# Three small tables at the start of a fused attention and mixture-of-experts kernel: other order, other queue, and four clears moved

## The chip, the cores and the metric

The kernel runs on one core of one Trainium2 chip. Its engines are TensorE (PE: matmuls, with weight loads shown apart as PEld), VectorE (DVE), ScalarE (ACT), GpSimd (POOL) and SyncE (SP, which here only issues transfers). The metric is the device time of one execution in microseconds; lower is better. Before the change it was 571.02 us, the median of three runs (569.08 to 572.53).

## The reference, cut to what matters

Three stages follow one another: an attention layer with a bias computed from positions, a token and channel mixer, and a layer of eight experts. The change touches the attention's start only, where the bias is prepared.

```python
scale = 1.0 / np.sqrt(D)                       # B, H, S, D = 2, 8, 576, 64; HID = 32
scores = scale * np.matmul(q, k.transpose(0, 1, 3, 2))
psi_rel = np.log1p(np.abs(pos[:, None] - pos[None, :]))
psi_i = np.log1p(np.maximum(pos[:, None], 1.0))
x = (psi_rel / psi_i)[..., None]
h = np.maximum(x @ w1 + b1, 0.0)               # w1: [1, 32], b1: [32]
bias = h @ w2                                  # w2: [32, 8]
scores = scores + bias.transpose(2, 0, 1)[None]
attn = softmax(scores)                         # then attn @ v
x = mixer(attn @ v); out = experts(x)          # two more stages, not touched
```

## The kernel before, in words

The bias is made in groups of 16 query rows. For each group, four "hidden" tiles of 128 x 576 hold max(distance x scale, -b1): line 497 on VectorE or GpSimd, line 494 on ScalarE. TensorE then multiplies them with `wblk`, a 128 x 32 block-diagonal copy of w2 (line 507), ScalarE copies the sum out and adds a constant (`ev`, line 510), and SyncE's queue writes it into the bias tile (lines 516 and 518). Five groups are made before the first scores. After them come 40 attention steps (scores, softmax, transposes, values), the mixer and the experts.

What all groups need is loaded in `load_const`:
- `tabs` (line 180): the table of distances with its scales, 128 rows of 848 numbers, 424 KB; its rest follows in line 186.
- `w1c`, `b1c` and `w2r` (lines 181 to 183): w1, b1 and w2, each repeated four times over the 128 partitions, so one number, one number and eight numbers a partition.
- From `w2r` GpSimd builds `wblk` (a clear in line 194, four copies in line 197).
- From `b1c` VectorE makes `negb` (line 464), from `tabs` and `w1c` it makes `sc` (line 465). All hidden tiles wait for these two.
- `bias_const` (lines 479 and 481) multiplies `wblk` with `b1c` and copies four constants out, between the hidden tiles of the first group and those of the second.

The order of the work is written out by hand. The lists in `ORDER` name the steps in the order of issue, and `ENGINE` says which engine takes which copy; each engine then runs its instructions in that order and waits where data is missing. Transfers of SyncE go to one DMA queue (q1 in the profile) in the order of issue, those of ScalarE to another (q10). SyncE also waits: each transfer signals one of eight semaphores in turn, and a transfer is issued only when the earlier one on the same semaphore has landed. So the tail of the first keys (line 227) is the first that can wait, for the transfer issued first on that semaphore.

`query_zero` (lines 297 and 298) clears the parts of the two query buffers `qt` that no later copy writes. In the kernel before it is the step "zero" of the list "start", between hidden3 and key_T01.

Of the kernel before, what the change touches and what calls it, by code (L numbers as in the profile page):

```python
# [21 lines left out]
B, H, S, D = 2, 8, 576, 64  # L22
# [32 lines left out]
QO = 3, 3, 3, 6  # L55

ORDER = {
    "start": "hidden0 const load_k2 tail_split0 hidden1 bias0 hidden2 bias1 key_T00 hidden3 zero key_T01 key_T11 key_T10 key_split0 tail_split1 bias2 hidden4 bias3 load_k4 hidden5 key_split1 tail_T bias4 load_v load_q".split(),
    "first": "scores0 hidden2 last_T prob_T0 values key_T0 tail_T hidden0 normalize query_T query_split hidden1 key_T1 bias_mm key_split out_T tail_split hidden3 query_rest".split(),
    "mixed": "hidden2 scores0 values tail_T hidden0 query_T normalize last_T prob_T0 key_T0 key_T1 query_split tail_split hidden1 key_split bias_mm query_rest out_T hidden3".split(),  # L60
    "bias": "query_T query_split hidden3 scores0 scores1 last_T values hidden0 query_rest hidden2 late bias_mm out_T mix prob_T0 prob_T1 hidden1 normalize".split(),
# [47 lines left out]
def body(ctx, tc, q, k, v, w1, b1, w2, wt1, wt2, wc1, wc2, wg, wl, mw1, mw2,  # L109
# [17 lines left out]
    with tc.manual_schedule():  # L127
        tok = ctx.enter_context(ExitStack())
        mix = TokenMix(nc, x)
        attention(tc, nc, tok, mix, q, k, v, w1, b1, w2, c_L, c_id, ident, x, wt1, wt2, prefill)  # L130
        if "x" in dbg:
            nc.sync.dma_start(dbg["x"], x)
        R = Routing(tc, nc, wg, wl, ident, c_tok, c_small, x2d, meta)
        X = Experts(tc, nc, R, Rings(tc, ctx, "big", side="right"), x_p, mw1, mw2, ident, x2d, meta, out)
        mixer(tc, nc, tok, mix, wc1, wc2, ident, x, R, X)
        if "x2" in dbg:
            nc.sync.dma_start(dbg["x2"], x2d)
        X.rest()
        X.close()
        R.close()  # L140


def attention(tc, nc, tok, mix, q, k, v, w1, b1, w2, c_L, c_id, ident, x, wt1, wt2, prefill):
# [10 lines left out]
    with ExitStack() as ctx:  # L154
# [8 lines left out]
        def alloc_ps():  # L163
            return ps_t.tile([128, 512], F32, name="tp", tag="tr")
# [3 lines left out]
        w1c = cst.tile([128, 1], F32, name="w1c")  # L168
        b1c = cst.tile([128, 1], F32, name="b1c")
        w2r = cst.tile([128, H], F32, name="w2r")  # L170
        wblk = cst.tile([128, 32], F32, name="wblk")

        def load_const():
            four = lambda ap, n: ap.rearrange("(a k) o -> a k o", a=1).to_broadcast([4, HID, n])

            cut = 4 * NG + S + 128
            warm = cst.tile([128, 1], F32, name="warm")
            nc.vector.memset(warm, 0.0)
            nc.scalar.activation(warm, warm, AF.Exp)
            nc.sync.dma_start(tabs[:, 0:cut], c_L[:, 0:cut])  # L180
            nc.scalar.dma_start(w1c, four(w1.rearrange("o k -> k o"), 1))
            nc.sync.dma_start(b1c, four(b1.rearrange("(k o) -> k o", o=1), 1))
            nc.sync.dma_start(w2r, four(w2, H))
            load_k(0)
            load_q(*steps[0])
            nc.sync.dma_start(tabs[:, cut:], c_L[:, cut:])
            nc.sync.dma_start(ident, c_id)

            zero = x[:, 0]
            nc.vector.memset(zero, 0.0)  # L190
            ps = alloc_ps()
            for _ in range(WARM):
                nc.tensor.matmul(ps, lhsT=zero[:, 0:128], rhs=zero, start=True, stop=True)
            nc.gpsimd.memset(wblk, 0.0)
            for ii in range(4):
                r = slice(32 * ii, 32 * ii + 32)
                nc.gpsimd.tensor_copy(wblk[r, 8 * ii:8 * ii + 8], w2r[r])
# [22 lines left out]
        def load_k(i):  # L220

            b, pr = divmod(i, NP)
            n = nat_p.tile([128, 20, D], F32, name="kn", tag="kn", bufs=2)
            main, hs = n[:, 0:16].rearrange("p (n h) d -> p n h d", h=4), k[b, 2 * pr:2 * pr + 4]
            for j in range(NIT):
                nc.sync.dma_start(main[:, j], hs[:, 128 * j:128 * j + 128].rearrange("h p d -> p h d"))
            nc.sync.dma_start(n[0:64, 16:20], hs[:, 512:S].rearrange("h p d -> p h d"))
            for j in range(2):
                nat["k", i + j] = main[:, :, 2 * j:2 * j + 2], n[0:64, 16 + 2 * j:18 + 2 * j]
# [14 lines left out]
        def load_q(it, i):  # L244

            b, pr = divmod(i, NP)
            n = nat_p.tile([128, 4, D], F32, name="qn", tag="qn", bufs=2)
            if it == NIT:
                tv = q[b, :, 512:S].rearrange("(a e) p d -> e p a d", e=2)
                for e in range(2):  # L250
                    nc.sync.dma_start(n[64 * e:64 * e + 64], tv[e])
                for j in range(NP):
                    nat["q", it, i + j] = n[:, j]
            else:
                nc.sync.dma_start(n, q[b, 2 * pr:2 * pr + 4, 128 * it:128 * it + 128].rearrange("h p d -> p h d"))
                nat["q", it, i] = n
# [37 lines left out]
        def query_zero():  # L294

            for qt in qts:
                nc.gpsimd.memset(qt[:, :, 0:2, 64:128].bitcast(F32), 0.0)
                nc.gpsimd.memset(qt[:, :, 2:4, 0:64].bitcast(F32), 0.0)
# [329 lines left out]
        def late_fetch(s):  # L628

            if pieces and any(f is decode for f, *_ in late.get(s, ())):  # L630
                fetch(pieces.pop(0))

        load_const()
        bias_setup()
        start = {
            "const": (bias_const,), "zero": (query_zero,), "load_k2": (load_k, 2), "load_k4": (load_k, 4), "load_v": (load_v, 0),
            "load_q": (load_q, *steps[NP]), "tail_T": (tail_T, *steps[0]),
        }
        for n in range(2):
# [1151 lines left out]
```

## Time and profile before

| | before |
|---|---|
| median of three runs | 571.02 us (569.08 to 572.53) |
| the profiled execution | 570.33 us |
| its span, first to last instruction | 568.3 us |
| TensorE busy | 543.3 us, 96% of the span |
| VectorE, ScalarE, GpSimd busy | 67%, 58%, 43% of the span |
| mean granted TensorE clock | 0.992 of full speed |

The span is what the trace covers; 2.0 us of the profiled execution lie around it. Times in the rows below are counted from the span's start. The part that the change touches lies before the first scores, which start 20.14 us after it.

### The profile page before, as it was taken

To read this page: it belongs to the slowest core of one execution; us is meant where nothing else is said; L and a number is where in the kernel's file an instruction comes from. 1 tells how busy PE (TensorE), PEld (TensorE's weight loads), DVE (VectorE), ACT (ScalarE), POOL (GpSimd) and SP (SyncE) were. 2 spreads that over 40 slices of the span, in tenths; PEclk is the share of its full clock that TensorE was granted. 3 is DMA by queue.
4 is the path that set the end of the run, shared out by engine and by line. 5 is a ranking of instruction groups with operands and counts; after the bars stand their busy time and mean duration, and the time that the engine had idled before them with its cause. 6 is when DMAs were issued, how large, how long until landed. Compare 5 with 4: busy or idle time off the path is not lost.

```text
span 568.3 us, 11965 instructions
## 1 busy us (share of the span) xinstructions
PE 543.3 (96%) x4306; PEld 429.5 (76%) x4306; DVE 380.7 (67%) x886; ACT 332.0 (58%) x622; POOL 243.9 (43%) x236
## 2 busy tenths in 40 slices
PE   7899999999999999999999989999999999999992
PEld 3566777777778987789999867787778778787872
DVE  6788798989987864899888247523582136668650
ACT  5799898799897862544444132223422457777760
POOL 4676656566772440244444202300034054657541
PEclk9899999999999999999999999999999999999998
DMA  6794785665754430344442030271003974576950
GB/s 163 181 198 118 172 188 140 175 147 128 165 128 118 113 111 2 100 129 148 150 151 72 0 93 1 54 284 33 20 19 118 400 273 129 168 240 223 372 187 14
DMA packets 72416, 79.92 MB, mean 141 GB/s; under 512 B 37126, under 2 KB 51724, under 8 KB 72348
## 3 DMA queue, kind: packets, MB, share of 16 engines
q1 hardware_dynamic: 68924, 73.80, 45.4%
q0 software_dynamic: 2176, 5.26, 2.7%
q8 instruction: 36, 0.59, 0.5%
q14 instruction: 32, 0.26, 0.2%
q10 hardware_dynamic: 1248, 0.01, 0.1%
HBM read 72.08 MB, written 5.34 MB: 136 GB/s over the span
## 4 chain that ended last, share of the span: by engine, by line
PE 74%; DVE 10%; ACT 6%; issue 4%; DMA 2%; POOL 2%; SPq 0%; POOLq 0%; DVEq 0%; ACTq 0%
PE ph L770 20%; PE po L770 15%; PE tp L436 7%; PE ps L370 6%; PE py L770 5%; PE ps L507 5%; PE tp L421 5%; PE tp L770 1%; DVE t L348 1%; PE tp L1476 1%; DVE K L282 1%; DVE raw L754 1%; DMA bias<-ev 1%; ACT t L351 1%; PE tp L452 1%
## 5 line engine op out<-in xcount | busy, mean ns | idle before, releaser
L497 POOL TENSOR_SCALAR hd<-tabs,sc,negb 128x576 f32<-128x576 f32 x32 | 76.3, 2388 | 3.1 <-PE tp L452 1.8
L770 PE MATMUL po<-cw,h 128*128 128x512 f32 x272 | 67.3, 396 | 0.0
L351 ACT ACTIVATE t<-t,st 128x576 f32<-128x576 f32 x72 | 55.4, 771 | 18.1 <-DVE st L348 17.7
L348 DVE CUSTOM_DVE_ANT_0 t<-ps,bias 128x576 f32<-128x576 f32 x72 | 52.2, 750 | 7.9 <-PE ps L370 5.2
L1439 DVE TENSOR_TENSOR big<-raw,big 128x1024 fp32r<-128x1024 f32 x30 | 42.5, 1438 | 22.2 <-ACT big L1438 22.1
L770 PEld LDWEIGHTS po<-cw,h 128*128 128x128 f32 x272 | 49.8, 188 | 10.0 <-issue 0.4
L370 PE MATMUL ps<-K,qt 128*128 128x288 f32 x320 | 54.8, 312 | 2.0 <-DVE qt L209 1.6
L436 PE MATMUL tp<-pt,v 128*64 128x128 f32 (+1 forms) x800 | 49.3, 268 | 0.0
L1217 POOL DMA_INDIRECT meta<-tokid,posi x10 | 10.0, 998 | 90.3 <-DVE tokid L1214 54.4
L370 PEld LDWEIGHTS ps<-K,qt 128*128 128x128 f32 x320 | 45.2, 192 | 4.0 <-POOL t L362 2.1
L770 PE MATMUL py<-big,hT 128*128 128x512 f32 x184 | 47.8, 400 | 0.4 <-POOL big L1439 0.4
L507 PE MATMUL ps<-hd,wblk 128*32 128x288 f32 x576 | 44.2, 412 | 2.5 <-DVE st L348 1.0
L1438 ACT CAST big<-raw 128x1024 fp32r<-128x1024 f32 x44 | 44.3, 1056 | 2.8 <-DMA big<-in_moe_w_dram 1.0
L436 PEld LDWEIGHTS tp<-pt,v 128*64 128x64 f32 x800 | 40.2, 137 | 7.4 <-issue 5.1
L770 PE MATMUL ph<-big,xT 128*128 128x512 f32 x168 | 42.9, 403 | 0.0
L497 DVE TENSOR_SCALAR hd<-tabs,sc,negb 128x576 f32<-128x576 f32 x69 | 42.3, 643 | 0.1
L762 POOL TENSOR_TENSOR big<-wf,big 128x512 fp32r<-128x512 f32 x12 | 18.7, 1558 | 51.1 <-ACT big L761 51.1
L770 PEld LDWEIGHTS py<-big,hT 128*128 128x128 f32 x184 | 33.8, 188 | 8.6 <-POOL big L1439 0.8
L494 ACT ACTIVATE hd<-tabs,b1c,sc 128x576 f32<-128x576 f32 x43 | 37.0, 866 | 3.8 <-DVE sc L465 3.7
L1439 POOL TENSOR_TENSOR big<-raw,big 128x1024 fp32r<-128x1024 f32 x10 | 27.6, 2763 | 24.3 <-ACT big L1438 24.3
L770 PEld LDWEIGHTS ph<-big,xT 128*128 128x128 f32 x168 | 30.6, 189 | 8.6 <-issue 1.6
L421 PE MATMUL tp<-ident,t 128*128 128x128 f32 x256 | 34.2, 275 | 0.0
(304 smaller groups left out, 1189.1 us busy)
## 6 DMA issues: line engine op xcount, KB each, us to landing
raw<-in_moe_w_dram SPq DMA_DIRECT2D x48, 512.0 KB
raw<-in_moe_w_ch_dram SPq DMA_DIRECT2D x24, 512.0 KB
bias<-ev SPq DMA_DIRECT2D x32, 288.0 KB
qt<-qs SPq DMA_DIRECT2D x64, 128.0 KB
lw<-in_moe_w_dram SPq DMA_DIRECT2D x16, 512.0 KB
big<-in_moe_w_dram SPq DMA_DIRECT2D x8, 512.0 KB
lw<-in_moe_w_dram SPq DMA_DIRECT2D x16, 256.0 KB
big<-in_moe_w_dram SPq DMA_DIRECT2D x16, 256.0 KB
```

What stands on the lines that cost most here:

```text
L348: nc.vector.tensor_tensor_reduce(t.rearrange("p (a j) -> p a j", a=2), ps[:, :, 0:HALF], bs.rearrange("p (a j) -> p a j", a=2), op0=ALU.ad ...
L351: nc.scalar.activation(t, t, AF.Exp, bias=st[:, j:j + 1], scale=-1.0, accum_out=st[:, 2 + j:3 + j])
L370: nc.tensor.matmul(ps[:, hf, 0:HALF], lhsT=qt[:, j], rhs=K[k][:, hf * HALF:(hf + 1) * HALF], start=j == pairs[0][0], stop=j == pairs[-1][0])
L421: nc.tensor.transpose(tp[:, 128 * j:128 * j + 128], tt[:, o:o + 128], ident)
L436: nc.tensor.matmul(po[64 * h:64 * h + 64, 0:rhs.shape[1]], lhsT=lhsT, rhs=rhs, start=j == 0, stop=j == 4)
L494: nc.scalar.activation(hd[:, qq], Lt[:, o:o + S], AF.Relu, bias=b1c, scale=sc[:, c])
L497: eng.tensor_scalar(hd[:, qq], Lt[:, o:o + S], sc[:, c], negb, ALU.mult, ALU.max)
L507: nc.tensor.matmul(ps[32 * qq:32 * qq + 32, hf, 0:HALF], lhsT=wblk, rhs=hd[:, qq, hf * HALF:(hf + 1) * HALF], start=True, stop=True)
L762: nc.gpsimd.tensor_tensor(lo, src, hi.bitcast(F32), ALU.subtract)
L770: nc.tensor.matmul(out, lhsT=lhs[a], rhs=rhs[b], start=first and i == 0, stop=last and i == 2)
L1438: nc.scalar.copy(hi, raw)
L1439: (nc.gpsimd if c == 3 and t else nc.vector).tensor_tensor(lo, raw, hi.bitcast(F32), ALU.subtract)
```

## The change

The transfer of `b1c` is issued first on SyncE's queue and `tabs` second. `w2r` leaves SyncE's queue for ScalarE's, behind `w1c`. `query_zero` is called at GpSimd's first instruction of the kernel, ahead of the clear of `wblk`, and no longer stands in the list "start".

```diff
-    "start": "hidden0 const load_k2 tail_split0 hidden1 bias0 hidden2 bias1 key_T00 hidden3 zero key_T01 key_T11 key_T10 key_split0 tail_split1 bias2 hidden4 bias3 load_k4 hidden5 key_split1 tail_T bias4 load_v load_q".split(),
+    "start": "hidden0 const load_k2 tail_split0 hidden1 bias0 hidden2 bias1 key_T00 hidden3 key_T01 key_T11 key_T10 key_split0 tail_split1 bias2 hidden4 bias3 load_k4 hidden5 key_split1 tail_T bias4 load_v load_q".split(),
...
             nc.vector.memset(warm, 0.0)
             nc.scalar.activation(warm, warm, AF.Exp)
+            nc.sync.dma_start(b1c, four(b1.rearrange("(k o) -> k o", o=1), 1))
+            nc.scalar.dma_start(w1c, four(w1.rearrange("o k -> k o"), 1))
             nc.sync.dma_start(tabs[:, 0:cut], c_L[:, 0:cut])
-            nc.scalar.dma_start(w1c, four(w1.rearrange("o k -> k o"), 1))
-            nc.sync.dma_start(b1c, four(b1.rearrange("(k o) -> k o", o=1), 1))
-            nc.sync.dma_start(w2r, four(w2, H))
+            nc.scalar.dma_start(w2r, four(w2, H))
             load_k(0)
...
                 nc.tensor.matmul(ps, lhsT=zero[:, 0:128], rhs=zero, start=True, stop=True)
+            query_zero()
             nc.gpsimd.memset(wblk, 0.0)
...
-            "const": (bias_const,), "zero": (query_zero,), "load_k2": (load_k, 2), "load_k4": (load_k, 4), "load_v": (load_v, 0),
+            "const": (bias_const,), "load_k2": (load_k, 2), "load_k4": (load_k, 4), "load_v": (load_v, 0),
```

On SyncE's queue the program begins with these transfers before the change (`kn` are the keys, `qn` the queries):

```order
L180 DMA tabs<-in_c_L_dram 128x848
L182 DMA b1c<-in_b_dram 128x1x1
L183 DMA w2r<-in_w_dram 128x1x8
L226 DMA kn<-in_k_dram 128x4x64 x4
L227 DMA kn<-in_k_dram 64x4x64
L251 DMA qn<-in_q_dram 64x4x64 x2
```

With the change they stand as follows; line numbers below line 193 are higher by one.

```order
L180 DMA b1c<-in_b_dram 128x1x1
L182 DMA tabs<-in_c_L_dram 128x848
L227 DMA kn<-in_k_dram 128x4x64 x4
L228 DMA kn<-in_k_dram 64x4x64
L252 DMA qn<-in_q_dram 64x4x64 x2
```

`b1c` went ahead of `tabs`, and `w2r` left; ScalarE now issues it directly behind `w1c`, and everything else on both engines keeps its order. On GpSimd the first work of the program before the change is this (`hd` is a hidden tile, `qm` the split queries):

```order
L194 MEMSET wblk 128x32
L197 COPY wblk<-w2r 32x8 x4
L203 CAST qm<-qn 128x2x64
L305 ISA
L305 TENSOR_TENSOR qm<-qn,qm 128x64
L497 TENSOR_SCALAR hd<-tabs,sc,negb 128x576
L297 MEMSET qt_104 128x2x2x64
L298 MEMSET qt_104 128x2x2x64
L297 MEMSET qt_105 128x2x2x64
L298 MEMSET qt_105 128x2x2x64
```

With the change it is this:

```order
L298 MEMSET qt_104 128x2x2x64
L299 MEMSET qt_104 128x2x2x64
L298 MEMSET qt_105 128x2x2x64
L299 MEMSET qt_105 128x2x2x64
L195 MEMSET wblk 128x32
L198 COPY wblk<-w2r 32x8 x4
L204 CAST qm<-qn 128x2x64
L306 ISA
L306 TENSOR_TENSOR qm<-qn,qm 128x64
L498 TENSOR_SCALAR hd<-tabs,sc,negb 128x576
```

The four clears moved ahead of everything that waits for a transfer. On TensorE and VectorE no instruction changes its place.

## Rows read from the trace of the kernel before

**Rows 1.** The page's first lines: span; busy time of each engine, share, instructions.

```profile
span 568.3 us, 11965 instructions
PE 543.3 (96%) x4306; PEld 429.5 (76%) x4306; DVE 380.7 (67%) x886; ACT 332.0 (58%) x622; POOL 243.9 (43%) x236
```

**Rows 2.** VectorE's timeline, 5 to 20: start us, us, instructions [idle before <-releaser].

```profile
5.51 0.15 DVE L464 TENSOR_SCALAR negb<-b1c 128x1 f32<-128x1 f32 x1 [4.06 <-DMA b1c<-in_b_dram]
5.60 0.29 DVE L465 TENSOR_SCALAR sc<-tabs,w1c 128x144 f32<-128x144 f32 x1
5.93 2.05 DVE L497 TENSOR_SCALAR hd<-tabs,sc,negb 128x576 f32<-128x576 f32 x4
7.91 0.44 DVE L481 COPY cb<-tp 128x1 f32<-128x1 f32 x4
...
14.41 0.46 DVE L282 TENSOR_TENSOR K<-tp,K 64x64 fp32r<-64x64 f32 x2 [0.49 <-ACT K L203]
14.90 2.89 DVE L497 TENSOR_SCALAR hd<-tabs,sc,negb 128x576 f32<-128x576 f32 x5
...
19.70 0.29 DVE L209 TENSOR_SCALAR qt<-tp 128x128 fp32r<-128x128 f32 x1
```

**Rows 3.** The chain of waits, 0 to 21: start us, us, what.

```profile
2.01 3.67 DMA w2r<-in_w_dram
...
7.59 0.43 PE tp L479 x32
...
20.14 0.89 PE ps L370 x3
```

**Rows 4.** SyncE's timeline, 0 to 12: transfers as they are issued.

```profile
0.76 0.39 SPq L180 DMA_DIRECT2D tabs<-in_c_L_dram  x1
1.21 0.75 SPq L182 DMA_DIRECT2D b1c<-in_b_dram  x1
2.01 0.54 SPq L183 DMA_DIRECT2D w2r<-in_w_dram  x1
2.59 2.88 SPq L226 DMA_DIRECT2D kn<-in_k_dram  x4
```

**Rows 5.** ScalarE's timeline, 0 to 21.

```profile
0.92 1.16 ACTq L181 DMA_DIRECT2D w1c<-in_w_dram  x1
...
5.93 1.63 ACT L494 ACTIVATE hd<-tabs,b1c,sc 128x576 f32<-128x576 f32 x2 [3.68 <-DVE sc L465]
```

**Rows 6.** DMA queues, 3.2 to 3.8 us: packets, MB, share of 16 engines.

```profile
q1 hardware_dynamic: 51, 0.05, 22.7%
q10 hardware_dynamic: 105, 0.00, 9.2%
```

**Rows 7.** DMA queues, 3.8 to 4.8 us.

```profile
q1 hardware_dynamic: 558, 0.11, 52.9%
q10 hardware_dynamic: 27, 0.00, 1.3%
```

**Rows 8.** DMA in all, 4.8 to 5.4 us.

```profile
DMA packets 379, 0.07 MB, mean 114 GB/s; under 512 B 379, under 2 KB 379, under 8 KB 379
```

**Rows 9.** DMA in all, 5.4 to 5.6 us.

```profile
DMA packets 115, 0.03 MB, mean 145 GB/s; under 512 B 115, under 2 KB 115, under 8 KB 115
```

**Rows 10.** GpSimd's timeline, 0 to 26.

```profile
5.82 1.73 POOL L197 COPY wblk<-w2r 32x8 f32<-32x8 f32 x4 [4.94 <-DMA w2r<-in_w_dram]
...
10.48 2.81 POOL L497 TENSOR_SCALAR hd<-tabs,sc,negb 128x576 f32<-128x576 f32 x1
13.25 0.30 POOL L297 MEMSET qt<- 128x256 f32 x1
...
15.68 2.78 POOL L497 TENSOR_SCALAR hd<-tabs,sc,negb 128x576 f32<-128x576 f32 x1 [0.72 <-ACT K L203]
```

**Rows 11.** Busy time by stretch: PE, PEld, DVE, ACT, POOL, granted clock, DMA.

```profile
18.50:20.10 1.60, 0.01 (x1) 0.00 (x0) 1.43 (x4) 0.94 (x3) 1.53 (x5) 1.00 0.76 209
20.10:23.70 3.60, 3.56 (x15) 3.15 (x15) 0.92 (x3) 1.47 (x3) 1.53 (x1) 0.54 0.90 207
```

## The prediction

> **What bounds the kernel now.** I read the page first. TensorE is busy for 96% of a span of 568.3 us [rows 1], so most of the time lies in 40 attention steps, the mixer and the experts, none of which this change touches. It moves work only in the stretch before the first scores, so that stretch is read by itself: VectorE's timeline, the chain of waits, the two issuing queues, and the packets of the DMA queues.
>
> VectorE does nothing for 4.06 us until b1c lands; negb starts at 5.51, sc at 5.60 and the four hidden tiles of the first group at 5.93 [rows 2]. ScalarE's hidden tiles wait for sc too [rows 5]. From there VectorE is almost never idle: the one gap on the way to the queries' copy at 19.70 is 0.49 us behind ScalarE [rows 2], which itself works through a list that began with sc. The first scores follow at 20.14 [rows 3]. So the first scores start about 14.6 us after negb, and what brings VectorE's start forward brings them forward, if nothing else holds.
>
> One other thing can hold. The chain of waits runs from w2r (issued at 2.01, landed 3.67 us later, at 5.68) through GpSimd's four copies, 5.82 to 7.55, to the 32 small matmuls at 7.59 [rows 3, 10]. VectorE needs the result of these for its four constants at 7.91, just as its first hidden tiles end, at 7.98 [rows 2]. The two paths, b1c to sc to the hidden tiles and w2r to wblk to the constants, arrive together. A gain needs both: if only b1c comes earlier, VectorE will wait at line 481 instead of line 464.
>
> **b1c ahead of tabs.** SyncE issues tabs from 0.76 to 1.15, b1c to 1.96 and w2r to 2.55 [rows 4]. b1c's packets stand in the same queue behind those of tabs, and at 3.2 to 3.8 that queue still moves 0.05 MB in 51 packets, so tabs ends in there; b1c and w2r trickle behind it. From 4.8 to 5.4, 379 packets average some 180 bytes (114 GB/s for 0.6 us, by 379), where the keys have 256 each; so about a third are small ones. From 5.4 to 5.6 they average 252, so the small ones have ended [rows 8, 9]. With the change b1c lands long before it is needed, and sc waits for the later of tabs and w1c.
> - tabs is issued later by b1c's issue and a gap, 1.21 + 0.75 - 1.15 - 0.02 = 0.79 us. If its last packet was at 3.6, it is now at 4.4. From the last small packet (5.4) to w2r's landing (5.68) are 0.3, so tabs lands at about 4.7.
> - w1c has the other queue: 105 packets from 3.2 to 3.8 and the last 27 before 4.8 [rows 6, 7]. With the same 0.3 it is there at 5.1 unless its company changes.
>
> So negb and sc could start at 5.1 in place of 5.51: 0.4 us. Bounds: with w1c through at 3.8 and tabs as above, 4.7, a gain of 0.8; and if tabs landed only when b1c did, which the trace can't exclude, sc comes at 5.51 + 0.79 = 6.3, a loss of 0.7 to 0.8. I take 0.4, since the rows on packets put the end of tabs well before 4.8.
>
> **w2r on ScalarE's queue.** ScalarE's issue of w1c ends at 0.92 + 1.16 = 2.08 [rows 5]; w2r then takes about its 0.54 of before, to 2.62, so it is issued no earlier than now (2.55). ScalarE has nothing else to do until 5.93. What changes is whom it stands behind: 128 packets of w1c, not 128 of tabs and 128 of b1c. At w1c's good rate (105 in 0.6 us) w2r needs 0.7 us; from 4.4, behind tabs, that ends at 5.1 and lands at 5.4, and from 3.8 it lands at 4.8. At w1c's poor rate (27 in 1.0 us, beside the keys of the other queue) 128 packets need 4.7 us: from 3.8 they end at 8.5 and w2r lands at 8.8. So between 0.9 us earlier and 3.1 us later; I take 0.3 to 0.4 earlier, since the good rate covers four fifths of the packets seen on this queue.
>
> The queue q10 carried 105 + 27 = 132 packets for w1c, 128 rows and four more [rows 6, 7]. The Trainium skill (DMA: Bandwidth & Descriptors, section "Issuing engines are not separate DMA queues") says that transfers of all issuing engines run on the same 16 DMA engines and that a second issuer saves only issue time. By that rule w2r would land at about 5.7 as before, and the gain would be nothing. The row on 4.8 to 5.4 leans its way: small packets pass slowly while keys share the engines [rows 8].
>
> On SyncE the 0.54 us of w2r and a gap go, and everything behind moves up by about 0.58. The four issues of keys, 2.88 us from 2.59 on [rows 4], then end near 4.9. Behind them the transfers wait on the semaphores of the first ones: the keys' tail now for b1c, the two of queries for tabs and w1c, and behind these stand the rest of tabs, the identity for the transposes and the next keys. With tabs at 4.7 and w1c at 5.1 no wait of theirs lasts; with a tabs at 6.3 the queries come about when they came before. So the queries land earlier by up to 0.6. GpSimd's hidden tile (10.48 to 13.29) starts earlier with them [rows 10], but VectorE's list at 14.90 does not wait for it [rows 2]: nothing on the path.
>
> **The four clears.** They take four times 0.30 us, overlapped to 1.06 in all, after GpSimd's hidden tile at 13.25. Moved to 0.75 they lie in the 4.94 us in which GpSimd waits for w2r, and end at about 1.9. If w2r landed before that they would cost; no row lets it. After 13.29 the next work comes 1 us earlier, but the hidden tile at 15.68 already waits 0.72 us for others [rows 10]; it will wait longer. Taken as nothing, at most 0.3 if that tile comes a little sooner.
>
> **The sum.** The gain is the smaller of the two paths': 0.4 us. Nothing after 20 us runs by a clock of its own, since transfers there wait for engines, so it is carried to the end: 570.33 - 0.4 = 569.9 us for the profiled execution. The median before lies 0.7 above that execution, so the median to expect is 570.6. A change of under 0.5%, 2.9 us, can't be told from none in this kernel, whose three runs differ by 3.5.
>
> **Rivals.**
> - *Nothing moves.* w2r keeps its landing near 5.7, since its small packets share DMA engines with tabs and keys in either queue, and VectorE only changes the line at which it waits. For it: the constants and the first hidden tiles end within 0.1 us of each other now. Against it: b1c's 128 packets no longer stand in front. Time: 570.3, median 571.0.
> - *Slower: w2r starves behind w1c.* In ScalarE's queue w2r alternates with keys of 256 bytes, where before the keys stood behind it in its own queue. It decides as soon as w2r lands after 5.7. At the poor rate it lands 3.1 us late, wblk ends at 10.7, and the whole chain is that much later: 573.4, median 574.1. Halfway between the rates the loss is 1.1 and the median 572.1. For it: w1c's stragglers. Against: most of w1c went fast while tabs was ending.
> - *The clock's stretch shifts.* TensorE has almost no work from 18.5 to 20.1, and for the next 3.6 us the granted clock is 0.54 on average, near its lower level of 1.2 GHz [rows 11]. Work at full clock would take about half; so 1.7 us go if the drop is gone, and as much is added by a second one. For it: GpSimd's and SyncE's earlier work changes when TensorE is fed. Against: the chain before 20 us keeps its order and its lengths. Times: 568.2 or 571.6, medians 568.9 or 572.3.
>
> **How the numbers follow.** A small gain as summed, 0.2 to 0.9 us: 0.45. Nothing moves: 0.27. Slower by w2r or by a late tabs: 0.18, a third of it beyond 2.9 us at the worst rate. The clock: 0.10, mostly toward a gain. The forecast is 570.6. Its own range, with the bounds of b1c's term and a run-to-run wander of 1.5 us, is 568.5 to 572.2; the clock on one side and half of the slow case on the other widen it to 567.9 to 572.9. Faster by over 0.5% takes the clock's gain, the sum and a lucky session together: 0.07. Slower by over 0.5% is the starved w2r, 0.06, and a little wander: 0.07. The rest, 0.86, is no change that can be told.
>
> **What would show it.** negb long before 5.5, and sc, not negb, as the instruction for which VectorE waits, at about 5.1. GpSimd's copies of wblk from about 5.4 and the constants without a wait. The four clears at 0.75 to 1.9. The first scores at about 19.7 and everything behind it shifted alike. I am wrong in the step on w2r if VectorE stands idle before line 481's copies, in the step on tabs if sc starts after 5.6, and in the carrying if the first scores come earlier and the span does not shrink.

## The result, and the profile after

| | before | after |
|---|---|---|
| median (lowest to highest, six runs each) | 570.17 us (569.08 to 572.53) | 575.01 us (573.19 to 575.77) |
| the profiled execution, its span | 570.33, 568.3 us | 575.48, 573.5 us |

Three more runs of the kernel before bring its median from 571.02 to 570.17. The ratio is 1.0076, with an interval of 1.0051 to 1.01 (ratios here and below are not quotients of the medians shown): the kernel became slower by 2.9 to 5.7 us. The forecast was 570.6, and its range ended at 572.9.

The page first, in the columns of [rows 1]. No engine has much more to do: TensorE is busy 0.2 us longer and GpSimd 1.9, in a span 5.2 us longer.

```profile
span 573.5 us, 11964 instructions
PE 543.5 (95%) x4306; PEld 428.4 (75%) x4306; DVE 381.2 (66%) x886; ACT 331.6 (58%) x622; POOL 245.8 (43%) x236
```

So most of the time is waiting. SyncE's timeline answers to [rows 4]: start, us, transfer.

```profile
0.75 0.76 SPq L180 DMA_DIRECT2D b1c<-in_b_dram  x1
1.57 0.42 SPq L182 DMA_DIRECT2D tabs<-in_c_L_dram  x1
2.04 3.26 SPq L227 DMA_DIRECT2D kn<-in_k_dram  x4
5.35 2.82 SPq L228 DMA_DIRECT2D kn<-in_k_dram  x1
8.61 1.26 SPq L252 DMA_DIRECT2D qn<-in_q_dram  x2
```

`tabs` is issued 0.81 us later than before, as foreseen. But the issue of the keys' tail lasts 2.82 us, where before it took 0.69. By the prediction's count it waits for `b1c`, which had landed before 4.39 (next rows), and the trace shows no wait ahead of it; what lengthens the issue itself it doesn't tell. Only the queries wait for a landing, that of `tabs`, and follow at 8.61 where they came at 6.25. SyncE's waits, 0 to 14 us (us in total, times, longest):

```profile
SPq L252 <- DMA tabs<-in_c_L_dram: 0.4, 1, 0.4
```

VectorE's timeline, to be read against [rows 2], says what was late.

```profile
4.39 0.15 DVE L465 TENSOR_SCALAR negb<-b1c 128x1 f32<-128x1 f32 x1 [2.94 <-DMA b1c<-in_b_dram]
8.62 0.29 DVE L466 TENSOR_SCALAR sc<-tabs,w1c 128x144 f32<-128x144 f32 x1 [4.08 <-DMA tabs<-in_c_L_dram]
8.95 2.05 DVE L498 TENSOR_SCALAR hd<-tabs,sc,negb 128x576 f32<-128x576 f32 x4
11.46 0.48 DVE L482 COPY cb<-tp 128x1 f32<-128x1 f32 x4 [0.46 <-PE tp L480]
```

`negb` comes 1.1 us earlier (5.51 to 4.39), which is what the change of order bought. Then VectorE waits 4.08 us for `tabs`, and `sc` starts at 8.62 instead of 5.60: 3.02 us later. A second, small wait of 0.46 us stands ahead of the constants. GpSimd's timeline, against [rows 10], explains it.

```profile
0.75 0.31 POOL L298 MEMSET qt<- 128x256 f32 x1 [0.29 <-POOLq L1785]
...
1.49 0.31 POOL L299 MEMSET qt<- 128x256 f32 x1
...
9.11 1.94 POOL L198 COPY wblk<-w2r 32x8 f32<-32x8 f32 x4 [7.25 <-DMA w2r<-in_w_dram]
```

The clears moved to an idle place. `w2r` landed at about 9, 3.3 us later than before. Both paths to the constants are thus late together, and either alone would have held them for about 3 us; they start 3.55 late (7.91 to 11.46), half a microsecond more than `sc`.

Why was `tabs` late? Each of its 128 rows is one packet of 424 KB / 128, 3.4 KB, while everything else there is under 512 bytes. So a stretch's packets "under 8 KB" less those "under 2 KB" are packets of `tabs`. Before the change, from 1.6 to 3.0 us (packets in all, then queue: packets, MB, share of 16 engines):

```profile
DMA packets 92, 0.31 MB, mean 223 GB/s; under 512 B 0, under 2 KB 0, under 8 KB 92
...
q1 hardware_dynamic: 92, 0.31, 74.1%
```

With the change, the stretches 1.6 to 2.6, 2.6 to 4.8, 4.8 to 6.2, 6.2 to 7.4 and 7.4 to 7.8, in this order:

```profile
DMA packets 39, 0.00 MB, mean 0 GB/s; under 512 B 39, under 2 KB 39, under 8 KB 39
...
q1 hardware_dynamic: 39, 0.00, 1.7%
...
DMA packets 178, 0.07 MB, mean 31 GB/s; under 512 B 158, under 2 KB 158, under 8 KB 178
...
q1 hardware_dynamic: 113, 0.07, 62.6%
q10 hardware_dynamic: 65, 0.00, 1.4%
...
DMA packets 450, 0.40 MB, mean 286 GB/s; under 512 B 354, under 2 KB 354, under 8 KB 450
...
DMA packets 1324, 0.33 MB, mean 278 GB/s; under 512 B 1315, under 2 KB 1315, under 8 KB 1324
...
DMA packets 306, 0.08 MB, mean 205 GB/s; under 512 B 303, under 2 KB 303, under 8 KB 306
```

Before, `tabs` ran alone, 92 packets in 1.4 us. With the change only b1c's packets move at first. From 2.6 to 4.8 just 20 packets of `tabs` pass, among 93 of b1c in its own queue (113 - 20) and 65 in ScalarE's (q10), w1c's. The bulk, 96, follows from 4.8 to 6.2. The last twelve trickle among the keys, nine from 6.2 to 7.4 and three from 7.4 to 7.8, and `sc` waits for them too: 1.6 us pass between the end of the bulk and the last packet, and no run takes this tail by itself. The share says how they waited: 62.6% of 16 engines for 2.2 us are 22 us of packet time; b1c's packets are short (those of 1.6 to 2.6 took 1.7% x 16 x 1.0 us / 39 = 7 ns each), so a packet of `tabs` was under way for about 1.1 us. Before it was 74.1% x 16 x 1.4 / 92 = 0.18 us. Few bytes move in that time (31 GB/s); the packets are held.

The hold does not last until all small packets are through. `w1c` is 132 packets (the last section says why), of which 65 had passed by 4.8; of the other 67, 47 pass by 6.2, beside the bulk (450 - 403).

Downstream, the windows of [rows 11] for this kernel (PE, PEld, DVE, ACT, POOL, granted clock, DMA):

```profile
6.90:11.10 4.20, 0.09 (x1) 0.00 (x0) 2.35 (x5) 1.62 (x2) 1.82 (x4) 0.95 0.56 118
11.10:15.00 3.90, 3.89 (x65) 1.87 (x66) 2.71 (x8) 0.74 (x1) 1.93 (x3) 0.61 0.92 216
...
24.40:28.00 3.60, 3.52 (x33) 2.63 (x34) 2.09 (x8) 2.24 (x6) 1.56 (x1) 1.00 0.87 200
```

TensorE has almost no work from 6.9 to 11.1, and in the next 3.9 us its granted clock is 0.61 on average, so mostly the level of 1.2 GHz. The low stretch that stood at 20.1 to 23.7 [rows 11] has no counterpart at the first scores: 24.4 to 28.0 has 1.00. TensorE's timeline shows both:

```profile
11.55 3.38 PE L508 MATMUL ps<-hd,wblk 128*32 128x288 f32 x32
...
24.48 1.31 PE L371 MATMUL ps<-K,qt 128*128 128x288 f32 x8 [1.62 <-DVE qt L210]
```

The first 32 matmuls of hidden tiles took 2.67 us before and take 3.38 now; the first eight of the scores took 2.09 and take 1.31. The first scores are 4.34 us late (20.14 to 24.48), the first softmax 3.56 (22.26 to 25.82). From there the shift is carried: 3.8 at 125 to 202 us, 4.0 at 210. In the profiled execution another 1.1 us or so are added between 505 and 530, in the experts, which the change doesn't touch; the ratio gives 4.3 in all.

### The profile page after: what moved, and what is told of

Same layout as the page of the kernel before. It is cut to its first block, busy times and chain, and to the rows that moved or that the text cites. A ratio compares the mean times of both kernels' runs of the same rounds, so it can differ in the third digit from the quotient of the medians.

```text
span 573.5 us, 11964 instructions
## 1 busy us (share of the span) xinstructions
PE 543.5 (95%) x4306; PEld 428.4 (75%) x4306; DVE 381.2 (66%) x886; ACT 331.6 (58%) x622; POOL 245.8 (43%) x236
## 4 chain that ended last, share of the span: by engine, by line
PE 68%; DVE 12%; ACT 7%; issue 5%; DMA 4%; POOL 2%; SPq 0%; POOLq 0%; ACTq 0%; DVEq 0%
PE ph L771 21%; PE po L771 16%; PE py L771 6%; PE ps L508 5%; PE tp L437 4%; PE ps L371 3%; PE tp L422 3%; ACT t L352 2%; DVE t L349 2%; DMA bias<-ev 2%; PE tp L771 1%; PE tp L1477 1%; DVE raw L755 1%; DVE K L283 1%; DMA w2r<-in_w_dram 1%
## 5 line engine op out<-in xcount | busy, mean ns | idle before, releaser
L1440 DVE TENSOR_TENSOR big<-raw,big 128x1024 fp32r<-128x1024 f32 x30 | 41.2, 1394 | 23.1 <-ACT big L1439 19.1
L508 PE MATMUL ps<-hd,wblk 128*32 128x288 f32 x576 | 45.4, 422 | 2.1 <-DVE st L349 1.0
L1440 POOL TENSOR_TENSOR big<-raw,big 128x1024 fp32r<-128x1024 f32 x10 | 26.3, 2632 | 23.0 <-ACT big L1439 22.9
```

Source lines behind the costliest of these rows:

```text
L508: nc.tensor.matmul(ps[32 * qq:32 * qq + 32, hf, 0:HALF], lhsT=wblk, rhs=hd[:, qq, hf * HALF:(hf + 1) * HALF], start=True, stop=True)
L1440: (nc.gpsimd if c == 3 and t else nc.vector).tensor_tensor(lo, raw, hi.bitcast(F32), ALU.subtract)
```

## The experiments

The theory from these rows: *a table of 128 one-number rows that is under way first holds the large transfer behind or beside it*. The rivals: w2r behind w1c on ScalarE's queue makes the loss; the clears do; the low clock does. The table collects what the runs gave (us from the span's start, one profiled execution each; "softmax" is how much later the one at 196.90 came; ratio with its interval). The column "softmax" holds more than the start: the kernel before has a stretch of low clock at 20 us that several of the runs lack, and e3, which changes nothing on the path, is 1.36 us ahead there. Differences of that size in the column say little.

| kernel | sc starts | wblk's copies | first scores | softmax | ratio |
|---|---|---|---|---|---|
| before | 5.60 | 5.82 | 20.14 | | 1 |
| after | 8.62 | 9.11 | 24.48 | +3.84 | 1.0076 (1.0051 to 1.01) |
| e1, b1c first alone | 7.64 | 7.91 | 24.20 | +3.42 | 1.0047 (1.003 to 1.0064) |
| e2, w2r's queue alone | 5.83 | 6.92 | 23.09 | +1.78 | 0.9998 (0.9984 to 1.0012) |
| e3, clears alone | 5.67 | 5.89 | 20.25 | -1.36 | 1.0001 (0.9984 to 1.0018) |
| e4, b1c in four parts | 6.86 | 4.72 | 21.19 | +0.32 | 1.0031 (1.0009 to 1.0054) |
| e5, w1c behind tabs | 6.35 | 6.78 | 21.95 | +1.78 | 1.0016 (0.9998 to 1.0034) |
| e6, tables of 32 rows, tabs first | 6.50 | 5.71 | 21.00 | -0.66 | 1.001 (0.9997 to 1.0022) |
| e7, tables of 32 rows, b1c first | 5.70 | 4.91 | 20.03 | -1.21 | 0.9978 (0.9961 to 0.9995) |
| e8, as e7, copies on GpSimd | 4.75 | 5.20 | 19.74 | -0.87 | 0.9963 (0.9944 to 0.9981) |
| e9, only b1 of 32 rows | 6.21 | 7.05 | 22.44 | +1.60 | 1.0028 (1.0009 to 1.0047) |

**e1_b1c_first: one part alone.** w2r stays on SyncE's queue and the clears stay where they were.

```diff
-            nc.sync.dma_start(tabs[:, 0:cut], c_L[:, 0:cut])
-            nc.scalar.dma_start(w1c, four(w1.rearrange("o k -> k o"), 1))
             nc.sync.dma_start(b1c, four(b1.rearrange("(k o) -> k o", o=1), 1))
+            nc.scalar.dma_start(w1c, four(w1.rearrange("o k -> k o"), 1))
+            nc.sync.dma_start(tabs[:, 0:cut], c_L[:, 0:cut])
             nc.sync.dma_start(w2r, four(w2, H))
```

> One part of the change alone: b1c ahead of tabs on SyncE's queue, w2r left on SyncE's queue, the clears left where they were. Theory A (b1c's 128 one-number packets stand at the head of SyncE's queue and hold tabs back behind them): tabs lands about as late as in the changed kernel, sc starts at 8 to 9 us in place of 5.6, the first scores come 3 to 4.5 us later than 20.14, and the time is 3 to 5 us above the kernel before. Theory B (w2r and w1c together on ScalarE's queue take the DMA engines that tabs needs): tabs is held only by the later issue, sc starts at 5.1 to 6.3 and the time is within 1 us of the kernel before.

VectorE's timeline of this run, and its window from 8.0 to 14.8 in the columns of [rows 11]:

```profile
7.64 0.29 DVE L465 TENSOR_SCALAR sc<-tabs,w1c 128x144 f32<-128x144 f32 x1 [3.23 <-DMA w1c<-in_w_dram]
```

```profile
8.00:14.80 6.80, 5.16 (x68) 2.52 (x68) 5.97 (x14) 2.94 (x4) 4.65 (x7) 0.50 0.80 185
```

With w2r in its old queue `sc` still starts 2.04 us late, and the time is up by 0.47%: most of the loss is in this one swap, though both figures are a little under those that theory A gave. The last to land is w1c here, on the other queue, so it isn't `tabs` alone that is late: b1c, w1c and `tabs` delay one another. Of the 4.06 us by which the first scores are late, `sc` explains half; in the low stretch that follows the wait (0.50 for 6.8 us) the first 32 matmuls of hidden tiles take 4.05 us in place of 2.67. The rest of the change's loss, 0.29%, belongs to no part by itself (e2 and e3 cost nothing), and the two intervals overlap.

**e2_w2r_act: the other part alone.**

```diff
-            nc.sync.dma_start(w2r, four(w2, H))
+            nc.scalar.dma_start(w2r, four(w2, H))
```

> The other part alone: w2r on ScalarE's queue behind w1c, tabs still issued first, the clears left where they were. Theory A: tabs lands as before, sc starts at 5.3 to 5.7; w2r lands anywhere from 5 to 7, so wblk ends at 7 to 9 and the time is from 0.5 us below to 1.5 us above the kernel before. Theory B: sc comes at 7 us or later and the time is 3 us or more above the kernel before.

VectorE's wait and GpSimd's, in this run:

```profile
8.85 0.44 DVE L481 COPY cb<-tp 128x1 f32<-128x1 f32 x4 [0.64 <-PE tp L479]
```

```profile
6.92 1.57 POOL L197 COPY wblk<-w2r 32x8 f32<-32x8 f32 x4 [6.05 <-DMA w2r<-in_w_dram]
```

w2r's copies start 1.1 us later and the wait ahead of the constants is there, as the slower rival had it. TensorE, idle for longer, then gets a clock of 0.57 from 8.5 to 12.5, and the first scores come 2.95 us late. Yet the time is unchanged: the low stretch at 20 us is gone (1.00 from 24 to 28), and the shift shrinks to 1.78 by 197 us and to 1.04 by 210. Its span is only 0.2 us longer in the end (568.5 beside 568.3). In which steps the delay of the first softmax (2.2 us) is given back stays open.

**e3_clears: the clears alone** (the change's edits to `ORDER` and `query_zero`, nothing else; cut to the call).

```diff
+            query_zero()
             nc.gpsimd.memset(wblk, 0.0)
```

> The third part alone: the four clears of the query buffers as GpSimd's first work, all transfers as in the kernel before. Both theories: they end at about 1.8 us, before w2r lands, and the first scores stay at 20.1 within 0.3 us; the time is within 0.5 us of the kernel before. Against both: a slowdown of 1 us or more would put part of the loss on GpSimd.

Nothing: 1.0001. The low clock at 20 us is absent in its profile, and the softmax comes 1.36 earlier, but the timed runs show no gain of that size.

**e4_b1c_four: the change, with b1c as four transfers of 32 rows.**

```diff
-            nc.sync.dma_start(b1c, four(b1.rearrange("(k o) -> k o", o=1), 1))
+            for a in range(4):
+                nc.sync.dma_start(b1c[32 * a:32 * a + 32], b1.rearrange("(k o) -> k o", o=1))
```

> The changed kernel with b1c loaded by four transfers of 32 rows in place of one of 128 rows whose outermost dimension is a repeat of four; all four still ahead of tabs, the same 128 packets of one number. Theory A in its narrow form (it is the few DMA engines that one such transfer uses that hold the queue): the packets spread over more engines, tabs starts to move about 0.6 us after its issue, which is 0.8 to 1.4 us later than in the changed kernel because of three more issues, and sc starts at 5 to 6.5 us in place of 8.6. Theory A in its wide form (128 one-number packets hold the queue wherever they go) and theory B: sc at 8.5 to 10 us and a time as in the changed kernel or above it.

SyncE's timeline, and the DMA in all from 2.8 to 4.4 and from 4.4 to 6.2:

```profile
0.75 2.03 SPq L181 DMA_DIRECT2D b1c<-in_b_dram  x4
2.82 0.65 SPq L183 DMA_DIRECT2D tabs<-in_c_L_dram  x1
```

```profile
DMA packets 316, 0.00 MB, mean 3 GB/s; under 512 B 316, under 2 KB 316, under 8 KB 316
...
DMA packets 396, 0.49 MB, mean 270 GB/s; under 512 B 269, under 2 KB 269, under 8 KB 396
```

Four issues take 2.03 us, so `tabs` goes out at 2.82. Until 4.4 only small packets of both queues pass, 316 of them, and none of `tabs`; its first packet comes 1.6 us after its issue, where in the kernel before it came within 1.04 us (issued at 0.76, one packet by 1.8). Then 127 of its 128 packets (396 - 269) pass in one stretch. So `tabs` waits here too, but once the small tables are through, its place behind them in the queue costs nothing more. `sc` at 6.86 is late by the late issue and by this wait, outside the ranges of both theories, and since b1c is spread and `tabs` is late at the same time, the run doesn't decide between them. The ratio, 1.0031, is more than the 1.05 us by which the first scores are late; the profile is that of the fastest of ten runs, 570.67 us with a median of 572.60, so it can't show the rest.

**e5_w1c_behind: b1c first, w1c behind tabs on SyncE's queue, against before.**

```diff
+            nc.sync.dma_start(b1c, four(b1.rearrange("(k o) -> k o", o=1), 1))
             nc.sync.dma_start(tabs[:, 0:cut], c_L[:, 0:cut])
-            nc.scalar.dma_start(w1c, four(w1.rearrange("o k -> k o"), 1))
-            nc.sync.dma_start(b1c, four(b1.rearrange("(k o) -> k o", o=1), 1))
+            nc.sync.dma_start(w1c, four(w1.rearrange("o k -> k o"), 1))
```

> b1c ahead of tabs as in the first experiment, but w1c no longer on ScalarE's queue beside it: it stands on SyncE's queue behind tabs, ahead of w2r. Theory A1 (b1c alone, by its 128 packets on few DMA engines, holds tabs until they have passed, near 4 us): the bulk of tabs (over 200 GB/s) still comes only from 3.8 to 5 us on. Theory A2 (tabs is held because two such transfers, b1c on one queue and w1c on the other, are under way at once): the bulk of tabs starts by 3.2 us, about 1 us after its issue. By both, sc waits for w1c, which now comes after tabs, at 6.5 to 8.5, and the time is 1 to 4 us above the kernel before.

DMA in all from 2.4 to 4.0, then from 4.0 to 4.4:

```profile
DMA packets 139, 0.09 MB, mean 53 GB/s; under 512 B 114, under 2 KB 114, under 8 KB 139
...
DMA packets 41, 0.14 MB, mean 348 GB/s; under 512 B 0, under 2 KB 0, under 8 KB 41
```

With w1c out of the way b1c alone holds `tabs`: 25 of its packets pass in 1.6 us beside 114 small ones, and as soon as these are through, 41 pass in 0.4 us. In the change the hold lasts to 4.8, with w1c's packets under way. The time of e5 itself can't be told from no change.

**e6_rows32: tabs first, all three tables as 32 rows, against before.** They follow one another on ScalarE's queue; VectorE copies w1 and b1 to the other three groups of partitions and builds `wblk`; the clears are first, as in the change.

```diff
-            nc.scalar.dma_start(w1c, four(w1.rearrange("o k -> k o"), 1))
-            nc.sync.dma_start(b1c, four(b1.rearrange("(k o) -> k o", o=1), 1))
-            nc.sync.dma_start(w2r, four(w2, H))
+            nc.scalar.dma_start(w1c[0:32], w1.rearrange("o k -> k o"))
+            nc.scalar.dma_start(b1c[0:32], b1.rearrange("(k o) -> k o", o=1))
+            nc.scalar.dma_start(w2r[0:32], w2)
...
+            for ii in range(1, 4):
+                nc.vector.tensor_copy(w1c[32 * ii:32 * ii + 32], w1c[0:32])
+                nc.vector.tensor_copy(b1c[32 * ii:32 * ii + 32], b1c[0:32])
...
-                nc.gpsimd.tensor_copy(wblk[r, 8 * ii:8 * ii + 8], w2r[r])
+                nc.vector.tensor_copy(wblk[r, 8 * ii:8 * ii + 8], w2r[0:32])
```

> A version to beat both: tabs first on SyncE's queue, and w1, b1 and w2 loaded once each to 32 partitions by transfers of 32 rows on ScalarE's queue; VectorE, idle then, copies them to the other three groups of partitions and builds wblk. The clears are GpSimd's first work. If the transfers with a repeat of four hold what stands behind them (theory A), then without them the keys follow tabs at full rate, w1, b1 and w2 land by 4.5, sc starts at 4 to 5 in place of 5.6, wblk is ready before it, and the first scores come 0.6 to 1.5 us earlier: 0.5 to 1.5 us below the kernel before. If small packets as such are slow whatever their spread, sc stays at 5.3 to 6 and the time within 0.5 us.

A miss. VectorE's timeline, and ScalarE's queue from 3.0 to 5.0:

```profile
4.47 0.14 DVE L197 COPY w1c<-w1c 32x1 f32<-32x1 f32 x1 [3.02 <-DMA w1c<-in_w_dram]
```

```profile
q10 hardware_dynamic: 144, 0.00, 4.0%
```

All 144 small packets pass from 3.0 on, though w1 was issued at 0.92; in e8 below its 48 pass from 2.0 to 2.8. What is under way first wins in this direction too: behind `tabs` the small tables wait, here as 32 rows on ScalarE's queue, in the kernel before as 128 rows on both. With the copies on top, `sc` comes at 6.50.

**e7_rows32_b1c_first and e8_rows32_wblk_pool: order and queues of the change, tables of 32 rows.** Against the change (e7):

```diff
-            nc.sync.dma_start(b1c, four(b1.rearrange("(k o) -> k o", o=1), 1))
-            nc.scalar.dma_start(w1c, four(w1.rearrange("o k -> k o"), 1))
+            nc.sync.dma_start(b1c[0:32], b1.rearrange("(k o) -> k o", o=1))
+            nc.scalar.dma_start(w1c[0:32], w1.rearrange("o k -> k o"))
             nc.sync.dma_start(tabs[:, 0:cut], c_L[:, 0:cut])
-            nc.scalar.dma_start(w2r, four(w2, H))
+            nc.scalar.dma_start(w2r[0:32], w2)
```

and the copies as in e6. e8 leaves those of `wblk` on GpSimd (`nc.gpsimd.tensor_copy(wblk[r, 8 * ii:8 * ii + 8], w2r[0:32])`).

> The changed kernel's order and queues (b1 ahead of tabs on SyncE's queue, w2 behind w1 on ScalarE's, the clears first) with the three small tables loaded to 32 partitions only and copied on by VectorE. Theory A in its narrow form: the order itself is harmless; tabs starts to move within 1 us of its issue and lands later than in the kernel before only by b1's issue, sc starts at 4.8 to 5.6, and the time is within 1 us of the kernel before. If any small transfer ahead of tabs holds it: sc at 7 or later and 1.5 us or more above the kernel before.

> The seventh experiment's kernel (all three tables loaded to 32 partitions, order and queues of the change) with the four copies that build wblk on GpSimd as before, so that VectorE no longer waits for w2 ahead of negb and sc. Expected: sc waits for tabs alone and starts at 4.4 to 5.0 in place of 5.70; wblk ends at 6.2 to 7.0, before the first hidden tiles do; the first scores come 0.6 to 1.2 us earlier than in that experiment, and the time is 1.5 to 2.8 us below the kernel before. If the start is then held by something else (keys, the identity, ScalarE), sc comes earlier but the first scores stay near 20.0, and the time is within 0.5 us of the seventh experiment's.

VectorE's timeline of e7:

```profile
2.73 0.14 DVE L197 COPY w1c<-w1c 32x1 f32<-32x1 f32 x1 [1.28 <-DMA w1c<-in_w_dram]
...
4.91 0.69 DVE L201 COPY wblk<-w2r 32x8 f32<-32x8 f32 x4 [1.54 <-DMA w2r<-in_w_dram]
5.63 0.15 DVE L468 TENSOR_SCALAR negb<-b1c 128x1 f32<-128x1 f32 x1
5.70 0.28 DVE L469 TENSOR_SCALAR sc<-tabs,w1c 128x144 f32<-128x144 f32 x1
```

The same order, now harmless: w1 and b1 are there at 2.73. But `negb` stands behind the copies of `wblk` in VectorE's list, which wait for w2. e8 takes these off VectorE. Its timeline, and the DMA from 2.0 to 2.8 and from 2.8 to 4.0:

```profile
3.41 0.15 DVE L468 TENSOR_SCALAR negb<-b1c 128x1 f32<-128x1 f32 x1
4.75 0.29 DVE L469 TENSOR_SCALAR sc<-tabs,w1c 128x144 f32<-128x144 f32 x1 [1.20 <-DMA tabs<-in_c_L_dram]
...
7.63 0.43 DVE L485 COPY cb<-tp 128x1 f32<-128x1 f32 x4 [0.49 <-PE tp L483]
```

```profile
q10 hardware_dynamic: 48, 0.00, 2.9%
...
DMA packets 234, 0.38 MB, mean 317 GB/s; under 512 B 128, under 2 KB 128, under 8 KB 234
```

The DMA moves 317 GB/s from 2.8, 106 packets of `tabs` among it in 1.2 us, and `sc` starts at 4.75, close to the 5.1 that was forecast for the change. e8, 568.73 us beside 570.15, beats the kernel before by its interval (0.9963, 0.9944 to 0.9981) and with it the change; from e7 it can't be told. Its gain, 2.1 us (1.1 to 3.2), is in the forecast's range of 1.5 to 2.8, but not by the forecast's path: the first scores come 0.29 us before those of e7 in place of 0.6 to 1.2, and 0.4 before those of the kernel before, and the span is 1.0 shorter. The constants wait 0.49 us for TensorE, and the rest of the gain is not explained.

**e9_b1c_rows32: the change, with only b1 as 32 rows.**

```diff
-            nc.sync.dma_start(b1c, four(b1.rearrange("(k o) -> k o", o=1), 1))
+            nc.sync.dma_start(b1c[0:32], b1.rearrange("(k o) -> k o", o=1))
...
+            for ii in range(1, 4):
+                nc.vector.tensor_copy(b1c[32 * ii:32 * ii + 32], b1c[0:32])
```

> The changed kernel with one thing mended: b1 goes to 32 partitions in one transfer of 32 rows, still ahead of tabs, and VectorE copies it to the other three groups. w1c and w2r stay on ScalarE's queue as transfers of 128 rows with the repeat of four. If only what stands in the same queue is held by such a transfer: the bulk of tabs (over 200 GB/s) moves by 3.0 us and sc starts when w1c has landed, at 4 to 5.5. If a transfer with the repeat holds the other queue too: the bulk of tabs comes only at 3.6 to 4.4, when w1c's packets have passed, and sc at 5.5 to 6.5. Either way the time is 2 us or more below the changed kernel's, if b1's packets are the main cause of its loss; if it stays within 1 us of the changed kernel's, they are not.

VectorE's timeline, and the queues from 2.4 to 4.0:

```profile
2.36 0.46 DVE L197 COPY b1c<-b1c 32x1 f32<-32x1 f32 x3 [0.92 <-DMA b1c<-in_b_dram]
6.21 0.29 DVE L468 TENSOR_SCALAR sc<-tabs,w1c 128x144 f32<-128x144 f32 x1 [3.20 <-DMA w1c<-in_w_dram]
```

```profile
q1 hardware_dynamic: 23, 0.08, 71.1%
q10 hardware_dynamic: 68, 0.00, 1.9%
```

b1 is out of the way at 2.36, and `tabs` is held all the same: 23 packets in 1.6 us, each under way for 71.1% x 16 x 1.6 / 23 = 0.79 us, while 68 of w1c's 132 packets trickle through the other queue. Unlike in the kernel before, `tabs` was issued at 1.21 here, 0.45 later, and met w1c's packets at the start. So the hold works across queues, and one table of 128 rows is enough. From 4.0 to 5.4 the other 105 packets of `tabs` pass beside 60 more of that queue: here too the hold ends before w1c is through.

## Why the prediction was wrong

**The bound, and the paths.** Right. The time is decided in the stretch before the first scores, on the two paths named, and both came late. Two of the marks set for an error came: "if sc starts after 5.6", and, on w2r, "if VectorE stands idle before line 481's copies" (0.46 us).

**b1c ahead of tabs: the step that failed.** "tabs is issued later by b1c's issue and a gap ... 0.79" held to 0.02 us; "so tabs lands at about 4.7" did not. It took for granted that `tabs` runs at its old pace wherever it starts. Measured: `sc` +3.02 us, against a forecast of -0.4 and a worst bound of +0.8. That bound supposed `tabs` landing when b1c does, at b1c's old landing plus the issue; it left out that w1c's packets would then pass at the same time too. It left out the last packets among the keys as well. [rows 6, 7] could have warned: w1c needed 1.6 us for its 132 packets on q10, and they ran only as `tabs` ended. No row showed `tabs` beside them, and for such a meeting the range had to be wider. e5 shows b1c's share of the hold, e9 w1c's, e4 and e8 that `tabs` runs freely once the small packets are through. Why a few small packets hold large ones stays open.

**w2r on ScalarE's queue.** The sign was wrong: 3.3 us later, not 0.3 to 0.4 earlier. The rival's poor rate had w2r landing at 8.8; it landed at about 9. That the two agree is luck: the rival had w2r's packets passing at 27 a microsecond from 3.8 on, but from 2.6 to 6.6 the queue moved 118 packets, fewer than w1c's 132, and from 6.6 to 8.6 it moved 146. The move was not what made the loss: alone it costs no time (e2). In the change it adds half a microsecond to a wait that `sc` had made, and in e1, in its old queue, w2r is late as well (its copies at 7.91). The Trainium skill (DMA: Bandwidth & Descriptors, section "Issuing engines are not separate DMA queues") was weighed as a reason for no effect. That transfers of two queues get in each other's way, as they may where they share engines, these traces show: e9's w1c holds `tabs` from the other queue. No effect does not follow from it, since e2's w2r lands 1.1 us later.

**SyncE.** Wrong by consequence: the queries came 2.36 us later instead of up to 0.6 earlier. They waited 0.4 us for `tabs`, as the prediction had counted the semaphores; the larger part is the issue of the keys' tail, 2.82 us, for which the prediction had no term and the trace names no cause.

**The clears.** Right: 0.75 to 1.8 (forecast 1.9), no effect (e3).

**The clock.** The rival took the old stretch's going and a new one's coming as alternatives, 1.7 us each; both came, at less than half that size. A new low stretch at 11 to 15 us cost 3.38 - 2.67 = 0.71, the old one's absence gave 4.34 - 3.56 = 0.78 back by the first softmax. Between them, nothing.

**The carrying.** Right in the change: 3.56 at the first softmax, 3.84 at 197 us, and a ratio of 4.3 us. The other runs show how loosely: e2's delay was returned, e4's loss is larger than the delay in its profile, and e3's lead of 1.36 us gave no gain.

## What to carry to other kernels

A table spread by a repeat in the transfer is cheap in bytes and was dear in company here: b1c beside `tabs` cost 0.47%. Have it through before a large transfer on the path starts, or start it when that one is through; which queue it is in did not save it (e9). Better was to load it once, as 32 rows, and copy it on chip: then a small transfer ahead cost its issue, 0.45 us (e7, e8). An outermost dimension of 128 rows in one transfer was not tried. When a forecast swaps two transfers, the delay of the second's issue is only the lower bound. For the upper one, let both run together at the pace of the slower; even that was short here, since `b1c` was through by 4.4 and the last packet of `tabs` passed after 7.4.

## What the runs showed of the hardware

A transfer has more packets than rows. The same table w1 is 132 packets as 4 x 32 rows (128 + 4) and 48 as 32 rows (32 + 16), the latter in e8's row. On the page, ScalarE's queue before and after the change, of each kernel its one row:

```profile
q10 hardware_dynamic: 1248, 0.01, 0.1%
```

```profile
q10 hardware_dynamic: 1380, 0.01, 0.1%
```

w2r's coming adds 132 as well. The Trainium skill (DMA: Bandwidth & Descriptors, section "Rules for kernel authors") says that a leading repeat of c copies confines a transfer to at most c engines, and advises an outermost dimension that is a multiple of 16. The four and the sixteen extra packets agree with it, if each engine in use adds one; no trace here names the engine of a packet.

What was not expected is that such a transfer slows another: a packet of 3.4 KB was under way for 1.1 us beside b1c and w1c and for 0.18 us alone. Whether the packets wait where they are made or in the engines, the traces don't say; nor do they tell the repeat of four from the mere number of rows, since e7 to e9 change both at once. Also open are what ends the hold while w1c is still under way, the long issue of the keys' tail, and the 1.1 us in the experts of the profiled execution.
